# Attention, Fourier mixing and a split-precision feed-forward on one core: an instruction order written out by hand, and feed-forward blocks of 512 tokens

## The chip, the core and the metric

The kernel runs on one core of a Trainium2 chip. A core has five engines that each run their own instruction queue in order: TensorE (PE; its weight loads are listed apart as PEld), VectorE (DVE), ScalarE (ACT), GpSimd (POOL) and SyncE (SP), which only issues transfers. Engines wait for each other by semaphores. Matmuls write to PSUM, which has eight banks of 512 fp32 values per partition; everything else lies in SBUF. The metric is the device time of one execution in microseconds (us). The kernel before took 1088.26 us, the median of 3 runs (1086.99 to 1090.42).

## What is computed

```python
def reference(q, k, v, w1, w2):        # B=8, H=8, S=576, D=64
    k_p = k.reshape(B, H, 72, 8, D).mean(axis=3)       # keys and values pooled by 8
    v_p = v.reshape(B, H, 72, 8, D).mean(axis=3)
    attn = softmax(q @ k_p.T / sqrt(D)) @ v_p
    x = attn.transpose(0, 2, 1, 3).reshape(B, S, 512)
    u = x + real(fft(fft(x, axis=1), axis=2))          # over tokens, then over channels
    un = (u - u.mean(-1)) / sqrt(u.var(-1) + 1e-6)
    return u + relu(un @ w1) @ w2                      # 512 -> 2048 -> 512, weights in fp64
```

There are 8 x 576 = 4608 tokens.

## The kernel before

**Two kinds of work.** For each batch `fe(b)`, here called the front end, does the attention, the two Fourier transforms as matmuls with cosine and sine tables, the sum u and the layer norm. It leaves four tiles for the feed-forward: `unh` and `unl` (high and low part of the centred u, 4 channel tiles), `U` (u itself) and `rb` (the factor of the norm, which is multiplied in at the end). These hold 1152 tokens, two batches, as a ring. `ffn(ro, nb, to, f0, f1)` (L705) then does a block of `nb` tokens.

**A step of the feed-forward.** Step f does 128 of the 2048 hidden channels with 24 matmuls of `nb` columns: 12 at L731 into a PSUM tile `g` (high parts, `unl` with the high weights, `unh` with the low weights, for 4 channel tiles each), then ACT writes `hh` (relu, rounded, L735), DVE writes `hl` (the rest, L736), and 12 at L715 add to four PSUM tiles `acc`. The `g` matmuls of the next step stand ahead of the `acc` matmuls of this one. After the last step of a block DVE does two passes per `acc` tile (L745, L746), and SP stores the result.

**Blocks.** `blocks()` (L71) names them in the order in which they run: batch 0 in two halves of 288 tokens, steps 0 to 7 of both and then 8 to 15 of both; batches 1 to 6 in nine blocks of 384 tokens with 16 steps each; batch 7 in two halves of 288 tokens. That makes 64 steps of 288 columns and 144 of 384.

**Weights.** They come as fp64 words. `prep_w(n)` (L178) turns a piece into a high and a low part: two ACT passes (L193, L195), two DVE passes (L198, L199), the high part by ACT (L203), the low part by POOL (L204), which is stored to DRAM (L205). Every step then loads its two low parts again (`load_low`, L211; SBUF has no room for all of them). The tiles for this are seven buffers under the tag `w`.

**Idle matmuls.** `keep_busy` (L223) has PE multiply the identity by itself, with numbers of repeats from the table `BUSY` (L58), 61 in all; each is two records in the trace.

**What sets the order.** A scheduler decides from a model of times how the instructions of the generators are laid into each engine's queue; `advance` and `need` say how far the front ends and the weights run ahead of the feed-forward, and `issue_after` ties single ones to others. The constant tables are loaded by POOL's queue (L129 `ca`, for the channels, 1157 KB; L130 `cb`, for the tokens, 1445 KB).

Of the kernel before, what the change touches and what calls it, by code (L numbers as in the profile page):

```python
# [29 lines left out]

NAT = {0, 1}

NM = {0, 1}
# [3 lines left out]
PK = {1, 2, 3, 4, 5, 6, 7}  # L37
PV = {0}

EL = {1}  # L40

HZ = {0, 1}

DG = {0, 1}


UE = [4, 1, 0]
UL = [3, 3, 2]

AHEAD, LEAD, PACE = 11, 12, 0.65  # L50

THIRD = 18

TAIL0, TAIL1, NEXT, STEPS = 10, 11, 20, 10
# [3 lines left out]
BUSY = {"start": 8, "S3": 3, "S2": 7, "S0": 9, "S1": 4, "T3": 3, "R": 4, "X": 12, "A": 3, "M": 8}  # L58
# [8 lines left out]
def slot(b):  # L67
    return ((b + 1) % 2) * S
# [15 lines left out]
def tile_kernel(ctx: ExitStack, tc: tile.TileContext, qt, kt, vm, vr, w1, w2, cad, cbd, mkd, out):  # L84
# [5 lines left out]
    wide = w1.dtype != F32  # L90

    wls = [dp.tile([P, NFC, DM], F32, name=f"w{i + 1}l") for i in range(2)]

# [39 lines left out]
    pieces = [(i, f, 0, 4, None) for f in range(12) for i in (0, 1)] + [(0, f, 0, 4, None) for f in range(12, 16)]  # L133
    pieces = [(i, f, c, w, n % (3 if THIRD <= n < 24 else 2)) for n, (i, f, c, w, _) in enumerate(pieces)] + [(1, 12, 0, 4, 1), (1, 13, 0, 4, 1)]
    pieces += [(1, f, c, 2, None) for f in (14, 15) for c in (0, 2)]

    after = {}
    for m, x in enumerate(pieces):
        same = [n for n in range(m) if pieces[n][4] == x[4]]
        if x[4] is None:  # L140
            after.setdefault(same[-2] if len(same) >= 2 else 26, []).append(m)
        elif m > 1:
            after.setdefault(same[-1] if same else m - 4, []).append(m)
    staged = {}

# [15 lines left out]
    def load_w(n):  # L161
        if n >= len(pieces):
            return
        i, f, c, w, place = pieces[n]
        src = (w1, w2)[i][:, f, c * P:(c + w) * P]
        if not wide:
            st = wk.tile([P, DM], F32, tag="w", bufs=7, name="wraw")[:, 0:w * P]
            nc.sync.dma_start(st, src)
            staged[n] = st
            return  # L170
        if place is not None:
            st = wk.tile([P, 2 * DM], I32, tag=f"tail{place}", name="wst")
        else:
            st = wk.tile([P, DM], I32, tag="w", bufs=7, name="wraw")
        nc.sync.dma_start(st, src.bitcast(I32))
        staged[n] = st.rearrange("p (c m w) -> p c m w", m=P, w=2)

    def prep_w(n):  # L178
        if n >= len(pieces):
            return  # L180
        i, f, c, w, _ = pieces[n]
        cl = slice(c * P, (c + w) * P)
        if wide:
            st = staged.pop(n)
# [12 lines left out]
            with tc.issue_after(behind["E", 0].ins) if n == 3 else ExitStack():
                nc.vector.tensor_scalar(out=dh[:, :, :, 1], in0=halves[:, :, :, 3], scalar1=0x8000, scalar2=None, op0=ALU.bitwise_and)  # L198
            nc.vector.scalar_tensor_tensor(out=di, in0=hi, scalar=3, in1=di, op0=ALU.logical_shift_left, op1=ALU.bitwise_or)  # L199
        else:  # L200
            d0 = staged.pop(n)
        wh = high(i, f)[:, cl]
        nc.scalar.copy(out=wh, in_=d0)  # L203
        nc.gpsimd.tensor_tensor(out=d0, in0=d0, in1=raw(wh), op=ALU.subtract)  # L204
        nc.sync.dma_start(wls[i][:, f, cl], d0)  # L205
        for m in after.get(n, ()):
            load_w(m)
# [3 lines left out]
    def load_low(i, n):  # L211

        lows[i, n] = t = wk.tile([P, DM], F32R, tag="w", bufs=7, name=f"w{i + 1}low")
# [5 lines left out]
    turn, behind = [0], {}  # L219

    idle = pp.tile([P, 512], F32, tag="acc3", name="idle")

    def keep_busy(n, ins=None):  # L223

        with tc.issue_after(ins.ins) if ins else ExitStack():
            for _ in range(n):
                nc.tensor.matmul(idle[:, 0:P], lhsT=ident, rhs=ident, start=True, stop=True)

    def bank(b, name, late=False):
        tag = "fe"  # L230
        if b == 0 and not late:

            tags = ["g1", "acc0", "fe", "g1", "acc1", "acc2", "fe"] if turn[0] < 24 else ["g1", "acc0", "g1", "acc1", "acc2"]
            tag = tags[turn[0] % len(tags)]
            turn[0] += 1
# [7 lines left out]

    keep_busy(BUSY["start"])


    def fe(b):
        ro = slot(b)
        Ub = U[:, :, ro:ro + S]
        Xb = Ub if b == 1 else X  # L250
# [43 lines left out]
        def prep_v(gi, i):  # L294
            g = GROUPS[gi][i]
            if i == 0:
                prep_rem(gi)
# [634 lines left out]
```

## Time and profile before

| what | value |
|---|---|
| median of 3 runs | 1088.26 us (1086.99 to 1090.42) |
| profiled execution, its own time | 1088.63 us |
| its span, first to last instruction | 1086.9 us |
| PE busy | 1044.1 us (96% of the span) |
| DVE, ACT, POOL busy | 609.4, 415.0, 249.4 us |
| mean granted clock of TensorE | 0.981 |

The profiled execution took 1.7 us more than its span, and 0.4 us more than the median. PE is busy nearly all the time, so the share of busy time alone says little: what matters is where PE is not busy, where its clock is granted at half, and how long one matmul takes when nothing else is in the way. The span falls into the stretch up to the first `g` matmul (0 to 77.5 us), one with the feed-forward of batch 0 and the front end of batch 1 (to 200.3 us), one up to the first block of 384 (to 244.5 us), the nine blocks of 384 (to 976.4 us), the two last blocks of 288, and the end.

### The profile page before, as it was taken

Reading aid. Unit: us, or ns where it says so; the run is one execution under the profiler, and the core shown is the slowest. Engines: PE = TensorE matmul, PEld = TensorE weight load, DVE = VectorE, ACT = ScalarE, POOL = GpSimd, SP = SyncE. Lnnn points to the kernel's source line nnn. Section 1 sums busy time; section 2 is a strip of 40 time slices with the busy share of each in tenths; the row PEclk is TensorE's granted clock in tenths of the full one; section 3 lists DMA queues with packets and bytes.
Section 4 is the critical chain, followed back from the end, with each engine's and each line's share of the span. In section 5 each row is a group of like instructions: output and inputs, shape, how many; then the busy total and the mean of one; then the engine's idle time right before and its main releaser. Section 6 shows DMA issues by size and latency. Waiting matters only on the chain.

```text
span 1086.9 us, 17702 instructions
## 1 busy us (share of the span) xinstructions
PE 1044.1 (96%) x6606; PEld 1018.9 (94%) x6606; DVE 609.4 (56%) x1237; ACT 415.0 (38%) x1102; POOL 249.4 (23%) x249
## 2 busy tenths in 40 slices
PE   8848898999999999999999999999999999999997
PEld 7737788999999999999999999999999999999997
DVE  7686878856376455756277455656467434522212
ACT  6767764543143341443233341443324422311110
POOL 4464355312240032201240122300331101300000
PEclk9878998999999999999999999999999999999999
DMA  7767976675445454445444454445435334446563
GB/s 246 259 215 249 330 253 213 191 201 165 127 122 162 123 167 133 128 141 162 139 122 147 140 155 132 135 125 156 158 108 157 97 107 123 115 131 185 166 187 99
DMA packets 91878, 175.80 MB, mean 162 GB/s; under 512 B 10128, under 2 KB 17296, under 8 KB 91536
## 3 DMA queue, kind: packets, MB, share of 16 engines
q1 hardware_dynamic: 91504, 172.01, 51.7%
q0 software_dynamic: 288, 2.66, 0.6%
q8 instruction: 52, 0.85, 0.3%
q14 instruction: 34, 0.28, 0.1%
HBM read 156.81 MB, written 17.83 MB: 161 GB/s over the span
## 4 chain that ended last, share of the span: by engine, by line
PE 85%; DVE 5%; DMA 4%; ACT 2%; POOL 2%; issue 1%; SPq 0%; DVEq 0%; POOLq 0%; ACTq 0%
PE acc L715 35%; PE g L731 35%; PE psX L432 3%; PE psS L345 3%; PE psP L592 2%; DMA k<-in_kt 1%; PE psA L547 1%; PE psB L575 1%; PE psT L385 1%; PE psQ L592 1%; DVE wd L199 1%; POOL k L280 1%; DMA w2l<-wd 1%; DVE wd L198 1%; PE psR L408 1%
## 5 line engine op out<-in xcount | busy, mean ns | idle before, releaser
L735 ACT ACTIVATE hh<-g 128x384 fp32r<-128x384 f32 (+1 forms) x208 | 96.2, 463 | 305.4 <-PE g L731 285.6
L736 DVE SCALAR_TENSOR_TENSOR hl<-g,hh 128x384 fp32r<-128x384 f32 (+1 forms) x208 | 108.6, 522 | 185.0 <-ACT hh L735 179.4
L715 PE MATMUL acc<-hh,w2h 128*128 128x384 f32 (+1 forms) x832 | 190.5, 329 | 0.2 <-DVE U L746 0.2
L715 PE MATMUL acc<-hh,w2low 128*128 128x384 f32 (+1 forms) x832 | 186.8, 327 | 0.3 <-DMA w2low<-w2l 0.3
L715 PE MATMUL acc<-hl,w2h 128*128 128x384 f32 (+1 forms) x832 | 182.3, 328 | 1.1 <-DVE hl L736 1.1
L731 PE MATMUL g<-unh,w1low 128*128 128x384 f32 (+1 forms) x832 | 178.2, 329 | 1.6 <-DMA w1low<-w1l 1.6
L731 PE MATMUL g<-unl,w1h 128*128 128x384 f32 (+1 forms) x832 | 177.8, 328 | 1.0 <-DVE unl L633 1.0
L731 PE MATMUL g<-unh,w1h 128*128 128x384 f32 (+1 forms) x832 | 175.6, 328 | 0.0
L715 PEld LDWEIGHTS acc<-hh,w2h 128*128 128x128 f32 x832 | 143.1, 189 | 2.6 <-ACT hh L735 0.7
L715 PEld LDWEIGHTS acc<-hh,w2low 128*128 128x128 f32 x832 | 144.0, 189 | 0.6 <-DMA w2low<-w2l 0.5
L715 PEld LDWEIGHTS acc<-hl,w2h 128*128 128x128 f32 x832 | 141.4, 190 | 2.1 <-DVE hl L736 1.7
L731 PEld LDWEIGHTS g<-unh,w1low 128*128 128x128 f32 x832 | 141.0, 190 | 2.0 <-DMA w1low<-w1l 1.8
L731 PEld LDWEIGHTS g<-unl,w1h 128*128 128x128 f32 x832 | 140.7, 190 | 1.4 <-DVE unl L633 1.3
L731 PEld LDWEIGHTS g<-unh,w1h 128*128 128x128 f32 x832 | 140.7, 191 | 1.3 <-issue 0.8
L364 POOL TENSOR_TENSOR t<-t,sm 128x720 f32<-128x720 f32 x32 | 47.0, 1469 | 284.6 <-DVE sm L363 247.3
L280 POOL TENSOR_TENSOR k<-k 128x288 f32<-128x288 f32 (+1 forms) x56 | 42.3, 755 | 97.1 <-DMA k<-in_kt 73.3
L624 POOL TENSOR_TENSOR U<-X,U 128x576 f32<-128x576 f32 (+1 forms) x14 | 20.0, 1433 | 124.9 <-DVE X L608 124.9
L345 PE MATMUL psS<-kpb,q 128*128 128x144 f32 x280 | 43.2, 289 | 3.8 <-DVE X L608 2.1
L345 PEld LDWEIGHTS psS<-kpb,q 128*128 128x128 f32 x280 | 39.8, 191 | 4.2 <-issue 2.3
L349 DVE TENSOR_REDUCE mx<-psS 128x6 f32<-128x432 f32 (+1 forms) x64 | 33.1, 525 | 18.9 <-PE psS L345 18.6
L360 ACT ACTIVATE t<-t 128x720 f32<-128x720 f32 x30 | 24.1, 804 | 37.3 <-DVE t L358 37.0
L745 DVE TENSOR_TENSOR acc<-acc,rb 128x384 f32<-128x384 f32 (+1 forms) x60 | 29.0, 518 | 13.8 <-PE acc L715 13.5
(209 smaller groups left out, 1425.7 us busy)
## 6 DMA issues: line engine op xcount, KB each, us to landing
w1low<-w1l SPq DMA_DIRECT2D x208, 256.0 KB, 2.7
w2low<-w2l SPq DMA_DIRECT2D x208, 256.0 KB, 2.9
wst<-in_w SPq DMA_DIRECT2D x30, 512.0 KB, 4.7
q<-in_qt SPq DMA_DIRECT2D x28, 288.0 KB, 3.1
k<-in_kt SPq DMA_DIRECT2D x28, 288.0 KB, 2.9
v<-in_vm SPq DMA_DIRECT2D x28, 256.0 KB, 3.0
out<-U SPq DMA_DIRECT2D x18, 384.0 KB, 3.5
w1l<-wd SPq DMA_DIRECT2D x16, 256.0 KB, 4.4
```

Of the source, the lines that this page charges most:

```text
L280: nc.gpsimd.tensor_tensor(out=out if n == 1 else src[:, :, 0:n], in0=src[:, :, 0] if n == 1 else src[:, :, 0:n], in1=src[:, :, 1] if n == ...
L345: mm = nc.tensor.matmul(ps[:, c * W2J:(c + 1) * W2J], lhsT=q[:, r0:r0 + P], rhs=kpb[g % 2], start=True, stop=True)
L349: nc.vector.tensor_reduce(out=mx[:, c0:c0 + n], in_=pv, op=ALU.max, axis=AX.X, negate=(b, g) in SM)
L360: nc.scalar.activation(t, t, AF.Exp, scale=1.0 / 64.0)
L364: ins = nc.gpsimd.tensor_tensor(out=t, in0=t, in1=sm.unsqueeze(3).broadcast_to([P, 5, 2, J]), op=ALU.mult)
L432: last = nc.tensor.matmul(ps, lhsT=w, rhs=a, start=(i == 0), stop=(i == len(mm) - 1))
L592: nc.tensor.matmul(ps, lhsT=w, rhs=a, start=(i == 0), stop=(i == 6))
L715: nc.tensor.matmul(acc[e], lhsT=w[:, e], rhs=h, start=(f == f0 and x == 0), stop=(f == f1 - 1 and x == 2))
L731: nc.tensor.matmul(ps, lhsT=w[:, c], rhs=x[:, ti, cl], start=(n == 0), stop=(n == 11))
L735: nc.scalar.activation(hh, ps, AF.Relu)
L736: nc.vector.scalar_tensor_tensor(out=hl, in0=ps, scalar=0.0, in1=raw(hh), op0=ALU.max, op1=ALU.subtract)
L745: nc.vector.tensor_tensor(out=acc[e], in0=acc[e], in1=rb[:, cl], op=ALU.mult)
```

## The change

**Blocks.** Batch 0 keeps its halves of 288 tokens, now with steps 0 to 3 of both, 4 to 7 of both, then a block of batch 1's first 512 tokens with all 16 steps, then steps 8 to 15 of both halves. Batches 2 to 7 follow with one block of 512 tokens each. The 64 tokens that each of the batches 1 to 7 leaves over are stored to DRAM by `keep_rest` (four transfers a batch) and loaded again by `load_rest`; they make the last block, of 448 tokens. That makes 32 steps of 288 columns, 112 of 512 and 16 of 448.

**Order.** Every generator yields after each single instruction. Each has a letter: `A` to `H` are parts of batch 0's front end and `a` to `h` those of batch 1's, `s` to `q` those of batches 2 to 7, `y` the feed-forward, `x` the loads of low parts, `L` and `1` to `4` the weights' load, ACT, DVE, copy and subtraction with its store. A string of some 3,000 entries says which goes next and by how many instructions, and this is the order on all five queues; the scheduler is off.

**Smaller edits.** 61 idle matmuls become 8, at the start. The pass tiles `wd` of the weights get 5 buffers of their own, the tag `w` has 8 instead of 7. The low parts of weights with f below 8 stay in SBUF for their first use. For batches 2 to 7 two of the four last additions of a block go from DVE to POOL. In batch 0's front end the additions and the norm are done half by half.

```diff
+NB = 512
+RM = S - NB
-AHEAD, LEAD, PACE = 11, 12, 0.65
-BUSY = {"start": 8, "S3": 3, "S2": 7, "S0": 9, "S1": 4, "T3": 3, "R": 4, "X": 12, "A": 3, "M": 8}
+ORDER = """
+i5 A1 i2 A1 G3 A2 B1 L1 A1 B2 G2 L1 B1 A1 i1 G1 B1 A3 B1 G4 A1 G2 A1 G1 A1 B1 G1 A1 G1 12 i1 11 A1 B1 11 B2 21 C1 A1 C1 21 C1 i1 B2 i1 E2 D1
...
+WD, RW = 5, 8
...
-    r = [(slot(0) + h * HS, HS, h * HS, f, f + 8) for f in (0, 8) for h in range(2)]
-    for m in range(3):
-        r += [(i * 384, 384, S + m * RING + i * 384, 0, NFC) for i in range(3)]
-    return r + [(slot(7) + h * HS, HS, 7 * S + h * HS, 0, NFC) for h in range(2)]
+    r = [(0, slot(0) + h * HS, HS, h * HS, f, f + 4) for f in (0, 4) for h in range(2)]
+    r += [(1, slot(1), NB, S, 0, NFC)]
+    r += [(0, slot(0) + h * HS, HS, h * HS, 8, NFC) for h in range(2)]
+    r += [(b, slot(b), NB, S + (b - 1) * NB, 0, NFC) for b in range(2, B)]
+    return r + [(B, slot(6), (B - 1) * RM, S + (B - 1) * NB, 0, NFC)]
...
     def load_consts():
         nc.gpsimd.dma_start(ca, cad)
+        yield
         nc.gpsimd.dma_start(cb, cbd)
+        yield
...
+            low = wk.tile([P, DM], F32R, tag="w", bufs=RW, name=f"w{i + 1}low") if f < 8 else d0.bitcast(F32R)
+            nc.gpsimd.tensor_tensor(out=low, in0=d0, in1=raw(high(i, f)[:, cl]), op=ALU.subtract)
+            yield
+            nc.sync.dma_start(wls[i][:, f, cl], raw(low))
+            if f < 8:
+                lows[i, f + f // 4 * 4] = low
...
-    keep_busy(BUSY["start"])
+    keep_busy(8)
+    def keep_rest(b):
+        cl = slice(slot(b) + NB, slot(b) + S)
+        for t, r in zip((raw(unh), raw(unl), U), rests):
+            nc.sync.dma_start(r[:, :, b - 1], t[:, :, cl])
+            yield
+        nc.sync.dma_start(rests[3][:, 0, b - 1], rb[:, cl])
+        yield
...
+            u = U[:, e, cl]
+            v = raw(gt(2 + e, "v"))[:, 0:nb] if e < 2 and b > 1 else acc[e]
+            nc.vector.tensor_tensor(out=v, in0=acc[e], in1=rb[:, cl], op=ALU.mult)
+            yield
+            (nc.gpsimd if e < 2 and b > 1 else nc.vector).tensor_tensor(out=u, in0=u, in1=v, op=ALU.add)
+            yield
...
+    with tc.manual_schedule(engines=ENG):
+        for x in ORDER.split():
+            for _ in range(int(x[1:])):
+                assert go(x[0], True)
```

Three places show what the order does. On DVE, the stretch between the last sums of batch 0's inverse transform (`X<-X,psP`) and its first `unl`. Before (`mx`, `sm` and `t_3_723` belong to batch 1's softmax, `wd` to the weights):

```order
L607 TENSOR_TENSOR X<-X,psP_2_546 128x2x287
L608 TENSOR_TENSOR X<-X,psP_2_546 128x2
L349 TENSOR_REDUCE mx<-psS_2_0_771 128x6
L361 TENSOR_REDUCE sm<-t_3_723 128x10
L349 TENSOR_REDUCE mx<-psS_2_3_783 128x4
L198 TENSOR_SCALAR wd<-wst 128x512
L624 TENSOR_TENSOR U<-X,U 128x288 x2
L617 TENSOR_TENSOR s<-X 128x288
L624 TENSOR_TENSOR U<-X,U 128x288
L617 TENSOR_TENSOR s<-X 128x288
L624 TENSOR_TENSOR U<-X,U 128x288
L198 TENSOR_SCALAR wd<-wst 128x512
```

And now (both `L1212` rows belong to the first half alone):

```order
L1150 TENSOR_TENSOR X<-X,psP_2_571 128x2x287
L1152 TENSOR_TENSOR X<-X,psP_2_571 128x2
L1184 TENSOR_TENSOR U<-X 128x288 x2
L1158 TENSOR_TENSOR U<-X,psQ_1_584 128x288
L1160 TENSOR_TENSOR U<-X,psQ_1_584 128x288
L1206 TENSOR_TENSOR U<-X,U 128x288
L1208 TENSOR_TENSOR U<-X,U 128x288
L1212 TENSOR_TENSOR X<-U,psM_0_616 128x2x288 x2
L1220 TENSOR_TENSOR unl<-X,unh 128x288 x3
L1206 TENSOR_TENSOR U<-X,U 128x288
L1208 TENSOR_TENSOR U<-X,U 128x288
```

Batch 1's softmax, the weights' passes and the second half's additions no longer stand ahead of the first half's `unl`. On PE, from the means `psM` of batch 0 into the first step of the feed-forward, before:

```order
L345 MATMUL psS_2_0_771<-kpb_75,q_2_758 128x144 x3
L345 MATMUL psS_2_3_783<-kpb_75,q_2_758 128x144 x2
L638 MATMUL psM_569<-s,avg 128x288
L638 MATMUL psM_580<-s,avg 128x288
L227 MATMUL idle<-ident 128x128 x8
L385 MATMUL psT_3_823<-ident,t_3_723 128x128 x4
L731 MATMUL g_0_0_1478<-unh,w1h 128x288
```

And now:

```order
L1171 MATMUL psM_0_616<-U,avg 128x288
L1171 MATMUL psM_1_618<-U,avg 128x288
L1303 MATMUL g_0_0_655<-unh,w1h 128x288 x4
L827 MATMUL psS_3_3_665<-kpb_80,q_3_279 128x144 x2
L1303 MATMUL g_0_0_655<-unl,w1h 128x288 x4
L1303 MATMUL g_0_0_655<-unh,w1low 128x288 x4
```

The eight idle matmuls and batch 1's transposes are gone from between them, and batch 1's scores `psS_2` come after. On POOL, around the loads of the constant tables, before:

```order
L364 TENSOR_TENSOR t_0_218<-t_0_218,sm 128x720
L129 DMA ca<-in_cad 128x2314
L130 DMA cb<-in_cbd 128x2890
L308 MEMSET wlo 32x128
L204 TENSOR_TENSOR wd<-wd,w1h 128x512
L308 MEMSET wlo 32x128
L364 TENSOR_TENSOR t_1_287<-t_1_287,sm 128x720
```

And now:

```order
L858 TENSOR_TENSOR t_1_256<-t_1_256,sm 128x720
L894 MEMSET wlo 128x128
L782 TENSOR_TENSOR k_3_216<-k_3_216 128x72x2
L236 TENSOR_TENSOR w1low<-wd,w1h 128x512
L939 MEMSET U 128x576
L782 TENSOR_TENSOR ks<-k_3_216 128x72
L894 MEMSET wlo 128x128
L169 DMA ca<-in_cad 128x2314
L236 TENSOR_TENSOR w2low<-wd,w2h 128x512
L171 DMA cb<-in_cbd 128x2890
```

Both loads stand behind the last normalisation of batch 0 (`t_1`) and behind one or two subtractions of the weights.

## Rows read from the trace of the kernel before

**Rows 1.** Windows by stage: bounds, length, then the columns of the first line

```profile
core 0: us, PE busy (x) PEld busy (x) DVE busy (x) ACT busy (x) POOL busy (x), PEclk, DMA share, GB/s
0.00:77.50 77.50, 54.31 (x326) 46.53 (x327) 55.67 (x116) 51.27 (x149) 37.01 (x52) 0.88 0.71 237
77.50:200.30 122.80, 109.34 (x687) 98.34 (x686) 96.73 (x189) 79.91 (x208) 61.34 (x60) 0.91 0.80 258
200.30:244.50 44.20, 44.20 (x340) 43.86 (x339) 26.09 (x68) 18.85 (x53) 7.11 (x5) 1.00 0.66 194
244.50:976.40 731.90, 731.90 (x4480) 726.18 (x4479) 406.80 (x811) 251.78 (x663) 143.97 (x134) 1.00 0.45 136
976.40:1080.60 104.20, 104.20 (x782) 104.01 (x780) 21.29 (x49) 13.15 (x32) 0.00 (x0) 1.00 0.56 163
1080.60:1086.90 6.30, 0.14 (x2) 0.00 (x0) 2.79 (x8) 0.00 (x0) 0.00 (x0) 0.93 0.29 94
```

**Rows 2.** Chain of waits in the blocks of 384: start, length, what, matmuls

```profile
959.80 2.10 PE g L731 x12
961.90 2.11 PE acc L715 x12
```

**Rows 3.** Chain of waits in the last blocks of 288

```profile
1031.38 3.17 PE g L731 x24
1034.55 3.19 PE acc L715 x24
```

**Rows 4.** PE's groups by line and form: busy, mean ns, idle before

```profile
L715 PE MATMUL acc<-hh,w2h 128*128 128x384 f32 x576 | 137.7, 340 | 0.0
L227 PE MATMUL idle<-ident 128*128 128x128 f32 x122 | 18.8, 315 | 1.8 <-POOL ident masks.py:199 1.8
```

**Rows 5.** ACT's and DVE's evictions by form, 244.5 to 1080 us

```profile
L735 ACT ACTIVATE hh<-g 128x384 fp32r<-128x384 f32 x144 | 70.3, 488 | 198.7 <-PE g L731 186.0 <-PE acc L715 11.7
...
L736 DVE SCALAR_TENSOR_TENSOR hl<-g,hh 128x384 fp32r<-128x384 f32 x144 | 79.7, 553 | 97.2 <-ACT hh L735 91.8 <-PE acc L715 3.4
```

**Rows 6.** Timeline of DVE, first sum and first low part of batch 0

```profile
36.64 0.94 DVE L444 TENSOR_TENSOR X<-psX,X 128x288 f32<-128x288 f32 x2 [1.35 <-PE psX L432]
...
76.97 1.47 DVE L633 TENSOR_TENSOR unl<-X,unh 128x288 fp32r<-128x288 f32 x1
```

**Rows 7.** Window between these two rows, columns as in Rows 1

```profile
36.64:76.97 40.33, 23.10 (x151) 19.89 (x150) 34.08 (x73) 25.37 (x76) 20.94 (x23) 0.86 0.64 203
```

**Rows 8.** DVE's groups by form, 36.6 to 77 us

```profile
L199 DVE SCALAR_TENSOR_TENSOR wd<-wst,wd 128x512 int32<-128x512 int32 x6 | 4.4, 728 | 0.0
L198 DVE TENSOR_SCALAR wd<-wst 128x512 uint16<-128x512 uint16 x7 | 3.7, 532 | 2.1 <-ACT wst L193 2.1
L644 DVE TENSOR_TENSOR X<-U,psM 128x1152 f32<-128x1152 f32 x2 | 2.5, 1307 | 0.0
L277 DVE TENSOR_REDUCE vs<-v 128x64 f32<-128x512 f32 x3 | 2.0, 672 | 0.0
```

**Rows 9.** Timeline of POOL around the loads of constants

```profile
22.00 1.22 POOL L129 DMA_DIRECT2D ca<-in_cad  x1
23.22 0.53 POOL L130 DMA_DIRECT2D cb<-in_cbd  x1
...
27.60 1.39 POOL L364 TENSOR_TENSOR t<-t,sm 128x720 f32<-128x720 f32 x1 [0.20 <-DVE sm L363]
```

**Rows 10.** Transfers: queue, KB, median us to landing

```profile
cb<-in_cbd POOLq DMA_DIRECT2D x1, 1445.0 KB, 9.7
```

**Rows 11.** Windows with the clock at half, columns as in Rows 1

```profile
62.00:68.80 6.80, 3.66 (x12) 3.04 (x13) 6.80 (x18) 2.06 (x4) 3.48 (x3) 0.50 0.47 181
72.30:85.90 13.60, 8.19 (x34) 7.82 (x35) 10.10 (x13) 11.29 (x36) 9.57 (x8) 0.50 0.60 188
```

**Rows 12.** Timeline of the end

```profile
1080.38 1.56 DVE L745 TENSOR_TENSOR acc<-acc,rb 128x288 f32<-128x288 f32 x4 [1.86 <-PE acc L715]
1081.85 1.53 DVE L746 TENSOR_TENSOR U<-U,acc 128x288 f32<-128x288 f32 x4
```

More of the change, by code (lines that the diff above doesn't have):

```diff
@@ L209, in tile_kernel @@
     lows = {}
     def load_low(i, n):
-        lows[i, n] = t = wk.tile([P, DM], F32R, tag="w", bufs=7, name=f"w{i + 1}low")
+        lows[i, n] = t = wk.tile([P, DM], F32R, tag="w", bufs=RW, name=f"w{i + 1}low")
         nc.sync.dma_start(raw(t), wls[i][:, steps[n]])
     steps = [f for *_, f0, f1 in blocks() for f in range(f0, f1)]
[L219 to L227, printed above, removed]
@@ L229, in bank, with keep_busy @@
-    def bank(b, name, late=False):
[L230 to L235, printed above, removed]
+    def keep_busy(n):
+        idle = pp.tile([P, 512], F32, tag="acc3", name="idle")
+        for _ in range(n):
+            nc.tensor.matmul(idle[:, 0:P], lhsT=ident, rhs=ident, start=True, stop=True)
+    def bank(b, name, late=False):
+        tag = "fe" if b or late else ("g1", "acc0", "g1", "acc1", "acc2", "acc3")[BANKS.index(name[2] + name[4:]) % 6]
@@ L700, in fe, with go @@
-        yield
+                    yield
+            yield 1
+        yield from steady(b, st, Xb, Ub, load, load_v, load_rem, prep_k, prep_v, scores, transposes, values, halves)
+    counts, streams = {}, {}
+    def go(x, fine=False):
+        traced = nc.cur_bb.bb.instructions
+        n = len(traced)
+        while True:
+            r = next(streams[x], 0)
+            if r == 1:
+                counts[x] = counts.get(x, 0) + 1
+            if r == 0 or (len(traced) > n if fine else r == 1):
+                return r != 0
@@ new lines, in loads, with weights @@
+    def loads():
+        for n in range(len(pieces)):
+            if pieces[n][4] in (2, 3):
+                pull("F", 3)
+            same = [m for m in range(n) if pieces[m][4] == pieces[n][4]]
+            if pieces[n][4] is None:
+                pull("2", 27 if len(same) < 2 else same[-2] + 1)
+            elif same:
+                pull("2", same[-1] + 1)
+            load_w(n)
+            yield
+            yield 1
+    def weights(k):
+        for n in range(len(pieces)):
+            pull("L123"[k], n + 1)
+            yield from prep_w(n, "ADCS"[k])
+            yield 1
@@ new lines, in ready, with feed @@
+    def ready(f):
+        pull("4", 1 + (2 * f + 1 if f < 12 else (28, 29, 31, 33)[f - 12]))
+    def feed():
+        for n, blk in enumerate(blocks()):
+            it = ffn(*blk)
+            last = 2 * (blk[5] - blk[4]) - 1
+            for h in range(last + 1):
+                pull("H", 20 if n or h > 1 else 18)
+                if h == last:
+                    pull("H", 25)
+                if blk[0] == 1:
+                    pull("h", 25 if h == last else 20)
+                while next(it) is None:
+                    yield
+                yield 1
+            assert next(it, 0) == 0
@@ new lines, in low_loads, with later, consts @@
+    def low_loads():
+        for n in range(len(steps)):
+            ready(steps[n])
+            for i in range(2):
+                if (i, n) not in lows:
+                    load_low(i, n)
+                    yield
+            yield 1
+    def later(b, *needs):
+        n = 0
+        for r in fe(b):
+            for a, x, m in needs:
+                if a == n:
+                    pull(x, m)
+            yield r
+            n += r == 1
+    def consts():
+        yield from load_consts()
+        yield 1
@@ new lines, in tile_kernel @@
+    streams.update({str(k + 1): weights(k) for k in range(4)}, L=loads(), x=low_loads(), y=feed(),
+        s=later(2, (0, "a", 6), (0, "b", 6), (0, "c", 6), (0, "d", 6), (0, "g", 4), (2, "h", 6), (4, "f", 7), (6, "h", 16), (10, "h", 25), (22, "y", 64)),
+        t=later(3, (0, "s", 22), (2, "s", 25), (6, "s", 29), (10, "s", 32)), u=later(4), v=later(5), p=later(6), q=later(7), r=load_rest(), k=consts(), l=first(), i=initial())
+    with tc.manual_schedule(engines=ENG):
+        for x in ORDER.split():
+            for _ in range(int(x[1:])):
+                assert go(x[0], True)
```

1371 lines of the change are left out of this document (942 added, 429 removed).

## The prediction, made before the changed kernel had run

> **What bounds the kernel now.** I read the windows by stage first [rows 1]. The columns to compare are PE's busy time with the length, and the clock: in the blocks of 384 (244.5 to 976.4) PE is busy 731.90 of 731.90 us at clock 1.00, and so it is from 200.3 on and in the last blocks of 288. There only PE work counts. Before that two stretches are loose: up to the first `g` at 77.5 us PE is busy 54.31 us, from 77.5 to 200.3 it is busy 109.34 of 122.80 us at a mean clock of 0.91, and there DVE is busy 96.73 us with 189 instructions, the most after PE.
>
> The second view is the chain of waits, for the price of one matmul. The mean of a record (340 ns [rows 4]) is no price, since the records overlap; the chain's pieces lie end to end: 12 + 12 matmuls of 384 columns take 2.10 + 2.11 us [rows 2], 175.4 ns each, and 24 + 24 of 288 columns take 3.17 + 3.19 us [rows 3], 132.5 ns each. The difference of 42.9 ns for 96 columns is 0.447 ns a column.
>
> With these prices the span is taken apart. The feed-forward is 64 steps x 24 x 132.5 ns = 203.5 us and 144 x 24 x 175.4 ns = 606.2 us, together 809.7. What the blocks of 384 leave over is front ends: 731.9 - 606.2 = 125.7 us for 4480 - 3456 = 1024 records [rows 1], 0.123 us a record. Of the profile's 6606 PE records 4992 are feed-forward and 122 idle [rows 4], so a front end has 1492 / 8 = 186.5 records or 22.9 us, and batches 1 to 7 take 160.3. Then 1086.9 = 77.5 (up to the first `g`) + 809.7 + 160.3 + 6.3 (the end [rows 1, 12]) + 33.1, and these 33.1 us are lost between 77.5 and 200.3: 122.8 - 109.3 = 13.5 us PE was not busy; a mean clock of 0.91 is half clock for 18% of the stretch, 22 us, in which some 11 us were lost; the last 8 or so I can't place.
>
> **The change part by part.**
>
> Width of the blocks. By 0.447 ns a column from 384 upward a matmul of 512 costs 232.6 ns and one of 448 204.0 ns (estimates; no row has these widths). New: 32 x 24 x 132.5 = 101.8, 112 x 24 x 232.6 = 625.2, 16 x 24 x 204.0 = 78.3, together 805.3 us: 4.4 less. Bounds: if what a matmul of 384 takes over its columns at the clock (175.4 - 384/2.4 = 15.4 ns) is a fixed sum, 512 costs 228.7 ns and 2688 of them 10.5 us less than I count; if the price is proportional (175.4 x 512/384 = 233.9), 3.5 us more. The line through both measured widths lies between, and I take it. So the wide blocks are worth little by themselves: PE streams the same columns, in fewer pieces.
>
> A step of 512 lasts 24 x 232.6 ns = 5.6 us. Its `hh` and `hl` (0.488 and 0.553 us at 384 [rows 5], some 0.65 and 0.74 at 512) fit under the 12 `acc` matmuls that stand between a `g` and its use, 2.8 us. ACT waited 186.0 us for `g` and DVE 91.8 us for `hh` [rows 5], so they have room; cost 0, and without this cover 1.4 us a step.
>
> The first `g`. Between DVE's first sum of batch 0 (36.64) and its first `unl` (76.97) [rows 6] DVE is busy 34.08 of 40.33 us with 73 instructions, 0.467 each [rows 7]. By the order 26 of them leave this stretch: 7 weight passes (4 x 0.532 + 3 x 0.728 = 4.3), 3 reductions (2.0), 12 of batch 1's softmax and 4 additions of the second half (16 x 0.467 = 7.5); the two subtractions of the mean get half as long (2.5 to 1.25) [rows 8]. Five passes become nine of half the length, which I count as nothing. That is 15.0 us less, 19.1 us busy. Idle time was 6.3 us; it grows, since a step that waits for PE or ACT (sine and cosine sums go DVE, ACT, PE, DVE in turn) now has less to fill it. If it stays 6.3, the first `g` comes at 36.6 + 19.1 + 6.3 = 62; if it grows to 17, at 73. I take 67, 10.5 us earlier. What is late next is the table `cb`: it was issued at 23.22 and takes 9.7 us [rows 9, 10]; now it stands behind the normalisation that ran at 27.6 [rows 9] and two subtractions, which I put at some 38 us. It lands at 48 then, about when the first transform back needs it; each us later than 50 costs one.
>
> The idle matmuls. 122 records become 16. They ran where PE had nothing else, so their 18.8 us [rows 4] give nothing back; what they may cost is a rival below. In two stretches with sparse matmuls the clock was at half although they were there, 62.0 to 68.8 (PE busy 3.66 of 6.80) and 72.3 to 85.9 [rows 11].
>
> The stretch up to batch 1's block. It holds 16 half-steps (24 x 132.5 ns x 16 = 50.9 us) and batch 1's front end (22.9): PE needs 73.8 us. By the order DVE has 175 instructions from the first `unl` to batch 1's last, where the old stretch has 189; at the old mean of 96.73 / 189 = 0.512 us these are 89.6 us, more than PE's. DVE bounds this stretch, and its length lies between 82 (the instructions are shorter than the mean) and 114 us (DVE is busy no more than 96.73 of 122.8, as before). I take 92, near the busy time, since the softmax of batch 1 and the weights' passes stand one by one between the evictions and no long wait of DVE is left that I can see in the order. Then 18 us are lost there and not 33.1.
>
> Low parts that stay, more buffers, two additions on POOL, `keep_rest` and `load_rest`. All lie beside PE: the reloads of low parts load the DMA engines at 0.45 in the blocks of 384, POOL is busy 143.97 of 731.9 us there [rows 1], and the last block is loaded long before. Cost 0; uncovered, a late `load_rest` would cost one round of transfers of some 5 us.
>
> The end. The last block has 448 columns instead of 288 and its additions are split between two engines; four products and four sums took 1.56 and 1.53 us [rows 12]. I leave 6.
>
> Sum: 67 + 805.3 + 160.3 + 18 + 6 = 1056.6 us of span, and 1.7 around it: 1058.3. The profiled execution was 0.4 us over the median, which I ignore.
>
> **The rivals.**
>
> *The loose stretch stays as loose.* DVE's queue is written now, and each instruction in it waits for its own input with all others behind it. If DVE is busy no more than before, the stretch lasts 114 us: 22 more, 1080. For it: the old order had waits of all kinds there. Against: what is in the way is moved off, and the low parts are in SBUF already. If the first `g` stays at 77 too, 1088 to 1091: no change.
>
> *A matmul has a fixed cost.* Then the 2688 matmuls of 512 take 228.7 ns, 10.5 us less: 1048. For it: nothing but that only two widths are measured. Against: the two give a slope of 0.447 ns, above 1/2.4 = 0.417. By the Trainium skill, "TensorE: Matmul & The Clock Gate", section "Back-to-back issue gap", a lone matmul at full clock takes its columns over 2.4 plus 2.5 ns. That would be 162.5 ns for 384, where the chain shows 175.4, so this trace does not agree; with its 215.8 ns for 512 the sum would be 45 us lower, and I give that no weight.
>
> *The clock stays at half: slower.* Rows 11 show half clock after sparse work. Without 53 idle matmuls PE does less from 15 to 67 us, and in the next stretch it waits for DVE. If the clock is at half for three quarters of the stretch, PE's 73.8 us become 129 (+37 on my 92), and the transforms on the way to the first `g` (23.10 us of PE work before [rows 7], about 8 us of it in DVE's way) come 8 us later: 1103. It decides against the change from 30 us more than I count, which is half clock in some two thirds of the stretch. Against: in the old stretch it was at half only 18% of the time with 13.5 us of idle PE, and the feed-forward's matmuls are dense whenever they run. The same page, section "What's actually happening", says that the throttled state is the default and activity releases it; the rows at 62 to 69 and 72 to 86 us agree, and by that rule the idle matmuls were worth something.
>
> *The written order stops PE in the steady part: slower.* An eviction behind a waiting front-end instruction on ACT or DVE would hold up `acc`. The room is 2.8 - 1.4 = 1.4 us a step; a wait of 0.3 us in each of 128 wide steps costs 38: 1096. Against: no idle time of PE from 200 to 1080 before [rows 1], and the front ends stand a block ahead of their use.
>
> **How the numbers follow.** The forecast gets 0.55, with its own range of 1043 to 1073 (first `g` 62 to 73, stretch 82 to 100, width -10.5 to +3.5). The loose stretch gets 0.18 (a third of it with no gain at the first `g`), the fixed cost 0.13, the clock 0.08, the stopped steady part 0.06. The range that leaves out no more than 2 in 10 reaches from 1038 (fixed cost with the shorter stretch) to 1081. Within 0.3% (3.3 us, about what can be told from no change here) lies the worst end of the loose stretch, 0.05; slower are the last two rivals but for their mild cases, 0.10; faster the rest, 0.85.
>
> **What would show it.** The first `g` at 62 to 73 us, and which wait stands before it (a wait for `cb` would be my step of the tables gone wrong). In the chain, 12 matmuls of 512 in 2.79 us (2.74 under a fixed cost). The first `g` of 512 columns at about 159 us, with DVE busy near 90 of the 92 us before it; at 180 it is the first rival. The windows with clock 0.50: some 20 us of them before 160, or over 50. From there on PE busy without a gap to the end. The prediction is wrong if PE waits in the steady part, or if the time before the first wide block is not shorter by 20 us or more for its work.

## The result, and the profile after

The changed kernel took 1057.71 us, the median of 4 runs (1057.01 to 1059.13), against 1089.34 us before (1086.99 to 1091.26, the three runs above and one more): a ratio of 0.9712, 95% interval 0.9688 to 0.9736. The forecast was 1058 us. The profiled execution took 1057.01 us with a span of 1055.3 us, so the sum of 1056.6 us of span was 1.3 us too high. That the sum fits this well is luck: the traces show below that terms were off by 3 to 9 us and cancel, and that one edit was priced at nothing which, in the changed order, the experiments price at some 18 us and more.

The windows by stage of the changed kernel, with the columns of [rows 1]; the bounds are the first `g` (58.8), the first `g` of 512 columns (148.2), the first of 448 (970.9) and the last matmul (1049.0):

```profile
0.00:58.80 58.80, 37.58 (x202) 30.75 (x202) 47.08 (x95) 39.61 (x109) 24.50 (x40) 0.90 0.73 252
58.80:148.20 89.40, 84.67 (x577) 78.97 (x578) 81.62 (x176) 69.37 (x197) 52.25 (x54) 0.97 0.72 245
...
148.20:970.90 822.70, 819.23 (x4188) 687.93 (x4187) 464.70 (x883) 291.68 (x742) 182.05 (x172) 1.00 0.40 130
970.90:1049.00 78.10, 78.06 (x385) 71.82 (x383) 13.90 (x23) 8.73 (x16) 2.52 (x3) 1.00 0.32 101
```

Against [rows 1] the stretch up to the first `g` is 18.7 us shorter, of the 31.6 us by which the whole span is. In the next one three engines are in heavy use: PE is busy 84.67 of 89.40 us at clock 0.97, DVE 81.62, ACT 69.37; before it was 109.34 of 122.80 at 0.91. From 148.2 us on PE is without work for 3.5 us only.

The price of a matmul, from the chain of waits at the change from 512 to 448 columns (start, length, what, matmuls):

```profile
959.85 2.79 PE acc L1289 x12
962.64 2.79 PE g L1303 x12
...
975.87 2.44 PE acc L1289 x12
978.31 2.43 PE g L1303 x12
```

2.79 / 12 = 232.5 ns for 512 columns (forecast 232.6) and 2.435 / 12 = 202.9 ns for 448 (204.0): the line through the two widths of [rows 2, 3] holds, and a fixed cost per matmul (228.7 ns) does not. No front end runs beside these steps.

What PE waited for, over the whole of the changed kernel (us in total, times, longest):

```profile
PE psA L1065 <- DMA ca<-in_cad: 4.8, 1, 4.8
PE g L1303 <- ACT unh L1217: 4.3, 1, 4.3
PE psT L926 <- POOL t L858: 4.2, 1, 4.2
PE psS L827 <- ACT kpb L801: 3.3, 4, 1.5
...
PE acc L1289 <- DVE U L1323: 1.5, 3, 0.6
```

No wait of the feed-forward for a low part is left. The longest wait is for the table `ca`, not `cb`, on the way to the first `g`. Of the waits shown, the first three and part of the fourth lie ahead of the first `g`.

The first row of batch 0's sums on DVE, its first `unl`, and between them two sums that are dear (start, length):

```profile
31.68 0.46 DVE L985 TENSOR_TENSOR X<-psX,X 128x288 f32<-128x288 f32 x1 [0.82 <-PE psX L967]
...
51.08 2.54 DVE L1184 TENSOR_TENSOR U<-X 128x288 f32<-128x288 f32 x2
...
58.90 1.19 DVE L1220 TENSOR_TENSOR unl<-X,unh 128x288 fp32r<-128x288 f32 x3
```

These answer to [rows 6]: the way from the first sum to the first `unl` is 27.2 us, not 40.3, and it also begins 5.0 us earlier.

### The profile page after: what moved, and what is told of

It is laid out like the page before. It is cut to its first block, busy times and chain, and to the rows that moved or that the text cites. A ratio compares the mean times of both kernels' runs of the same rounds, so it can differ in the third digit from the quotient of the medians.

```text
span 1055.3 us, 14747 instructions
## 1 busy us (share of the span) xinstructions
PE 1019.5 (97%) x5348; PEld 869.5 (82%) x5348; DVE 609.1 (58%) x1177; ACT 409.4 (39%) x1062; POOL 262.5 (25%) x269
## 4 chain that ended last, share of the span: by engine, by line
PE 81%; DVE 10%; POOL 3%; ACT 2%; DMA 2%; issue 1%; SPq 0%; DVEq 0%; POOLq 0%; ACTq 0%
PE g L1303 34%; PE acc L1289 34%; PE psS L614 3%; PE psX L694 2%; PE psP L287 2%; PE psA L396 1%; DVE wd L227 1%; PE psB L412 1%; PE psQ L287 1%; PE psT L651 1%; DMA ca<-in_cad 1%; DVE wd L225 1%; DMA k<-in_kt 1%; PE psA L1065 1%; POOL t L858 0%
## 5 line engine op out<-in xcount | busy, mean ns | idle before, releaser
L1310 DVE SCALAR_TENSOR_TENSOR hl<-g,hh 128x512 fp32r<-128x512 f32 (+2 forms) x160 | 101.1, 633 | 217.4 <-ACT hh L1308 216.8
L1308 ACT ACTIVATE hh<-g 128x512 fp32r<-128x512 f32 (+2 forms) x160 | 88.3, 552 | 293.6 <-PE g L1303 292.7
L1289 PE MATMUL acc<-hh,w2h 128*128 128x512 f32 (+2 forms) x640 | 170.5, 376 | 2.2 <-DVE U L1323 1.5
L1289 PE MATMUL acc<-hl,w2h 128*128 128x512 f32 (+2 forms) x640 | 168.0, 373 | 0.0
L1289 PE MATMUL acc<-hh,w2low 128*128 128x512 f32 (+2 forms) x640 | 167.9, 373 | 0.0
L1303 PE MATMUL g<-unh,w1h 128*128 128x512 f32 (+2 forms) x640 | 162.9, 376 | 4.3 <-ACT unh L1217 4.3
L1303 PE MATMUL g<-unl,w1h 128*128 128x512 f32 (+2 forms) x640 | 162.4, 375 | 0.3 <-DVE unl L1220 0.3
L1303 PE MATMUL g<-unh,w1low 128*128 128x512 f32 (+2 forms) x640 | 162.5, 376 | 0.0
L1289 PEld LDWEIGHTS acc<-hh,w2h 128*128 128x128 f32 x640 | 113.9, 188 | 21.6 <-DVE U L1323 2.5
L1289 PEld LDWEIGHTS acc<-hh,w2low 128*128 128x128 f32 x640 | 115.0, 188 | 19.0
L553 POOL TENSOR_TENSOR k<-k 128x288 f32<-128x288 f32 (+1 forms) x48 | 31.7, 660 | 54.4 <-DMA k<-in_kt 29.9
L621 ACT ACTIVATE t<-t 128x720 f32<-128x720 f32 x24 | 19.3, 805 | 41.4 <-DVE t L619 41.4
```

The costliest lines, as they stand in the source:

```text
L553: nc.gpsimd.tensor_tensor(out=out if n == 1 else src[:, :, 0:n], in0=src[:, :, 0] if n == 1 else src[:, :, 0:n], in1=src[:, :, 1] if n == ...
L621: nc.scalar.activation(t, t, AF.Exp, scale=1.0 / 64.0)
L1289: nc.tensor.matmul(acc[e], lhsT=w[:, e], rhs=h, start=(f == f0 and x == 0), stop=(f == f1 - 1 and x == 2))
L1303: nc.tensor.matmul(ps, lhsT=w[:, c], rhs=x[:, ti, cl], start=(n == 0), stop=(n == 11))
L1308: nc.scalar.activation(hh, ps, AF.Relu)
L1310: nc.vector.scalar_tensor_tensor(out=hl, in0=ps, scalar=0.0, in1=raw(hh), op0=ALU.max, op1=ALU.subtract)
```

## The experiments

All were timed against the kernel before. Its medians beside these runs were 1088.15 to 1088.43 us, against 1089.34 beside the changed kernel, so a difference of about 1 us between two runs says little. Differences are of medians from the changed kernel's 1057.71 us.

**The scheduler decides again.** Blocks, buffers and kept low parts stay.

```diff
-    with tc.manual_schedule(engines=ENG):
+    with ExitStack():
```

> The changed kernel with the scheduler deciding each engine's order again; blocks, buffers and kept low parts stay as changed. Theory (the written order brings the gain, by the first g at 58.8 us and the packed stretch of 89.4 us up to the first block of 512): the first g comes at 68 to 80 us, the first block of 512 starts at 165 to 190 us instead of 148, and the time is 1072 to 1095 us. Rival (the new blocks and the kept low parts bring it, the order is only a way to write it down): within 5 us of the changed kernel's 1057.7.

Measured: 1156.64 us, 99 us more (ratio to before 1.0628, 1.0596 to 1.066). The first `g` came at 86.5 us, the first block of 512 at 195.1.

```profile
0.00:86.50 86.50, 47.71 (x217) 38.33 (x217) 66.10 (x126) 57.63 (x166) 39.38 (x61) 0.74 0.73 248
86.50:195.10 108.60, 87.81 (x564) 78.98 (x564) 85.59 (x174) 63.45 (x171) 51.54 (x49) 0.92 0.58 197
195.10:1075.00 879.90, 849.91 (x4211) 711.51 (x4211) 447.40 (x858) 281.63 (x712) 171.50 (x158) 0.96 0.38 115
```

The last row ends a little into the last block. The new blocks alone are not the gain; without the written order they come out slower than the kernel before. But the loss is larger than either theory said, and 52 of the 99 us arise after the first block of 512 has begun (PE is idle for 30 us there, and its mean granted clock is 0.96). The generators were rewritten to be laid out by the string, and it may be that their plain text is no good order for the scheduler; that was not tested. So this run shows that the new kernel needs its written order, not by how much that order beats the old one.

**The low parts go through DRAM again.** The low parts of weights with f below 8 are stored and reloaded for their first use also. The loads are issued where the step asks for them.

```diff
-            low = wk.tile([P, DM], F32R, tag="w", bufs=RW, name=f"w{i + 1}low") if f < 8 else d0.bitcast(F32R)
+            low = d0.bitcast(F32R)
...
-            if f < 8:
-                lows[i, f + f // 4 * 4] = low
```

> The changed kernel in which every low part is stored and loaded again, also for its first use (16 parts, 32 transfers more in the stretch up to the first block of 512). Theory (DVE binds that stretch, the transfers lie beside it): -1 to +2 us. Rival (the stretch is dense because the low parts are in SBUF): PE's g waits for w1low again, and the time is 6 us or more longer.

Measured: 1075.48 us, 17.8 more (0.9885, 0.9863 to 0.9908). My theory falls: PE waited 14.2 us for them, and the first block of 512 began at 165.5 us, 17.3 later. The wait in total, and then the longest of the three with the transfers that SP issued ahead of it:

```profile
PE g L1301 <- DMA w1low<-w1l: 14.2, 3, 8.7
107.25 6.21 SPq L205 DMA_DIRECT2D wst<-in_w  x2
113.55 0.38 SPq L238 DMA_DIRECT2D w1l<-wd  x1
114.03 0.38 SPq L246 DMA_DIRECT2D w1low<-w1l  x1
118.53 1.33 PE L1301 MATMUL g<-unh,w1low 128*128 128x288 f32 x4 [8.67 <-DMA w1low<-w1l]
```

The load of the low part (L246) was issued at 114.03 us and was there when PE went on at 118.53. Ahead of it in SP's queue stood a store and two loads of weights' words (L205), the second of which waited until 113 us. SP waited little for stores in this run, 3.8 us at L246. So the loss could have come from issuing the loads late, and the next run issues each right behind its store:

```diff
-                lows[i, f + f // 4 * 4] = low
+                load_low(i, f + f // 4 * 4)
```

> The changed kernel in which the 16 low parts are again stored and loaded back for their first use, but each load is issued by SP directly behind its store, long before the step that needs it (in the run before, the loads were issued where the steps stand, and it took 17.8 us more). Theory (the loss there came from loads that were issued late; transfers as such lie beside PE): 0 to 4 us longer than the changed kernel's 1057.7. Rival (the way through DRAM costs whenever it is taken, since SP waits for each store to land, some 3 to 4 us, with the other loads queued behind it): 8 to 18 us longer.

Measured: 1085.64 us, 27.9 more (0.9976, 0.9965 to 0.9988): more than either theory said, and nearly the whole gain is gone. Issuing early is worse than issuing late. The waits of SP's queue up to 180 us in this run:

```profile
SPq L248 <- DMA w2l<-wd: 38.0, 8, 11.0
SPq L248 <- DMA w1l<-wd: 32.7, 8, 5.6
```

L248 is the load of a low part. It waits for the store to land, 70.7 us in 16 waits, 4.4 us each, and every transfer behind it in SP's queue waits too: ACT then waited 19.3 us for `wst`, the weights' words, in the stretch (0.7 in the changed kernel), and the first `g` itself was 6.6 us late. The last run of the three copies the low part by a transfer from SBUF to SBUF, so that bytes, transfers and buffers are as in the run before but nothing waits for a store:

```diff
-                lows[i, f + f // 4 * 4] = low
+                lows[i, f + f // 4 * 4] = t = wk.tile([P, DM], F32R, tag="w", bufs=RW, name=f"w{i + 1}low")
+                nc.sync.dma_start(raw(t), raw(low))
```

> The run with the loads issued at once, but each low part is copied by a transfer from the tile in SBUF and not loaded back from DRAM: the same 16 transfers of 256 KB into the same buffers, without SP's wait for the store to land (which was 38.0 + 32.7 us for 16 stores there). Theory (SP's wait in the written order is what costs, with the weights' loads queued behind it): 0 to 4 us longer than the changed kernel's 1057.7. Rival (the extra transfers, or the buffers that are held longer, cost): 10 us or more longer.

Measured: 1061.01 us, 3.3 more (0.9743, 0.9724 to 0.9763). Of SP's waits for stores 3.1 us are left of 70.7, and the longest items are now the subtraction itself, which the stores waited for anyway, and a pass of DVE:

```profile
SPq L238 <- POOL wd L236: 35.3, 15, 6.7
SPq L205 <- DVE wd L227: 28.2, 10, 6.4
```

So 24.6 of the 27.9 us go with SP's waits (the transfers behind them and the low parts themselves come late), and about 3 with the transfers and buffers. That the load has to wait for the landing is what the Trainium skill states in "DMA: Bandwidth & Descriptors", section "Two DMAs through the same engine are not ordered": only the completion semaphore of the first orders a second that depends on it. SP waits in this way in the run with the loads issued at once; the price, 4.4 us for each of 16, is that run's.

**More work for DVE, for ACT and for PE, in the stretch from the first `g` to the first block of 512.** Each run adds instructions to one engine there, and changes nothing else in the program.

```diff
+            for _ in range(2 if 9 <= n < 27 else 1):
                 nc.vector.tensor_scalar(out=dh[:, :, :, 1], in0=st.bitcast(U16)[:, :, :, 3], scalar1=0x8000, scalar2=None, op0=ALU.bitwise_and)
```

> The changed kernel with one of DVE's two passes issued twice for 18 pieces of the weights (those prepared from 66 to 145 us): 18 x 0.46 to 0.7 us = 8 to 12 us more of DVE's work in the stretch of 89.4 us in which it is busy 81.6. Theory (DVE binds the stretch): the first block of 512 starts 5 to 12 us later and the time is 5 to 12 us longer. Rival (PE's 84.7 busy us or the chain of dependences bind it, and DVE's 7.8 idle us take the passes up): 0 to 3 us longer.

```diff
+            for _ in range(2 if 9 <= n < 27 else 1):
                 nc.scalar.activation(dh[:, :, :, 0], st.bitcast(U8)[:, :, :, 3], AF.Copy, scale=1.0 / 32.0, bias=-15.5 / 32.0)
```

> The changed kernel with one of ACT's two passes issued twice for the same 18 pieces: 18 x 0.66 to 0.78 us = 12 to 14 us more of ACT's work in the stretch in which it is busy 69.4 of 89.4 us. Theory (DVE binds, ACT has 20 us of room): 0 to 5 us longer. Rival (ACT is as much in the way, by the order of its queue): 8 to 14 us longer.

```diff
+                    for m in range(6 if b == 0 and f < 8 and n == 0 else 1):
-                    nc.tensor.matmul(ps, lhsT=w[:, c], rhs=x[:, ti, cl], start=(n == 0), stop=(n == 11))
+                        nc.tensor.matmul(ps, lhsT=w[:, c], rhs=x[:, ti, cl], start=(n == 0), stop=(n == 11 or (b == 0 and f < 8 and n == 0 and m < 5)))
```

> The changed kernel with the first matmul of each of the 16 early half-steps of batch 0 issued six times instead of once: 80 x 132.5 ns = 10.6 us more of PE's work in the stretch up to the first block of 512 (PE is busy 84.7 of 89.4 us there). Theory (PE, ACT and DVE are each near full, so that any of them lengthens the stretch by what is added): 7 to 11 us longer. Rival (DVE and ACT bind it and PE follows): 0 to 4 us longer.

| run | added to the engine | time | more than the changed kernel | ratio to before |
|---|---|---|---|---|
| DVE twice | 11.9 us (93.5 for 81.6) | 1068.05 | 10.3 | 0.9816 (0.9792 to 0.9839) |
| ACT twice | 13.1 us (82.5 for 69.4) | 1067.65 | 9.9 | 0.9806 (0.9784 to 0.9827) |
| PE more | 10.6 us (80 matmuls at 132.5 ns) | 1062.43 | 4.7 | 0.9763 (0.9743 to 0.9782) |

The stretch in the first two runs, with the columns of [rows 1], DVE's run first, and then ACT's:

```profile
59.00:159.00 100.00, 90.03 (x574) 83.85 (x575) 93.51 (x192) 69.19 (x197) 52.25 (x54) 0.91 0.67 218
```

```profile
59.00:159.00 100.00, 89.11 (x579) 82.53 (x580) 81.83 (x178) 82.54 (x215) 50.32 (x54) 0.93 0.65 219
```

DVE's work comes out nearly whole, as the theory had it. ACT's does too, against the theory: it had 20 us of idle time and took up only 3 of the 13. Idle time between the waits of a queue in fixed order was no room for more work here. PE, the busiest of the three, took up about half, which lies between the two theories. So all three bind; DVE and ACT alike, as far as these runs can tell them apart, and PE less.

Two things limit this. A part of the price is the clock: for as many matmuls as before PE is busy 90.03 and 89.11 us in these rows instead of 84.67, at a mean granted clock of 0.91 and 0.93 instead of 0.97. So some 4 to 5 of the 10 us are PE's own work at half clock, between longer waits. And both doubled passes stand in the one chain that prepares a weight (ACT, DVE, ACT, POOL), so a fuller engine is not told apart from a longer chain; in neither run, though, does the feed-forward wait for a weight in this stretch.

**The table `ca` earlier.** POOL issues it ahead of the normalisation of `t_0`.

```diff
-D1 a1 C1 E2 12 21
+D1 a1 k1 C1 E2 12 21
...
-a1 G2 k1 41 31 L1
+a1 G2 41 31 L1
```

> The changed kernel with the load of ca moved up in POOL's queue, ahead of the normalisation of t_0, so that it is issued at about 21.5 us instead of 30.6. Theory (PE's wait of 4.8 us for ca lies on the way to the first g): the wait is gone, the first g comes 2 to 4 us earlier, the time is 2 to 4 us shorter. Rival (the transfers already run at 300 to 400 GB/s from 20 to 33 us, so ca pushes other loads back, and DVE's own queue is as late): -1 to +3 us.

Measured: 1056.24 us, 1.5 less (0.97, 0.9682 to 0.9718, which overlaps the changed kernel's interval), between what the two theories said. The wait for `ca` is gone, but the first `g` came at 58.5 us, 0.3 earlier: PE waits for ACT's `unh` in its place.

```profile
PE psA L1062 <- ACT unh L1008: 4.6, 2, 3.9
PE g L1300 <- ACT unh L1214: 4.3, 1, 4.3
```

**Idle matmuls again in the two waits.** 16 ahead of the first `psA` and 14 ahead of the first `g`.

```diff
+    def busy_again():
+        for n in (16, 14):
+            idle = pp.tile([P, 512], F32, tag="acc1", name="idle")
+            for _ in range(n):
+                nc.tensor.matmul(idle[:, 0:P], lhsT=ident, rhs=ident, start=True, stop=True)
+            yield
```

> The changed kernel with idle matmuls again in PE's two long waits on the way to the first step: 16 ahead of the first psA (wait of 4.8 us) and 14 ahead of the first g (wait of 4.3 us). Theory (taking them out cost nothing, DVE and ACT are in the way): -1 to +1 us. Rival (the clock at half from 40 to 43 and from 58 to 63.5 us holds PE up, and the idle matmuls give it back): the clock stays at full there, 2 to 4 us shorter.

Measured: 1056.90 us, 0.8 less (0.9712, 0.9692 to 0.9731): no difference. In the changed kernel the clock is at half just behind these waits (0.52 from 40 to 43 us, and the first two rows below). In this run it is 1.00 in both places and falls only later, to 0.77 and 0.73, behind 3.4 us in which PE was busy for 1.21 us (61.2 to 64.6). The first `g` comes 1.0 us earlier, at 57.86, but the first block of 512 does not: 148.37 us against 148.24. The changed kernel first, then this run:

```profile
57.80:61.20 3.40, 2.37 (x9) 2.23 (x10) 3.37 (x7) 2.52 (x6) 1.34 (x2) 0.50 0.00 0
61.20:64.60 3.40, 3.40 (x18) 3.40 (x18) 3.37 (x6) 0.78 (x3) 1.03 (x2) 0.59 0.02 5
```

```profile
64.60:68.00 3.40, 2.12 (x9) 1.89 (x10) 3.40 (x8) 3.33 (x9) 2.32 (x3) 0.77 0.34 91
68.00:71.40 3.40, 3.40 (x22) 3.40 (x21) 3.40 (x6) 1.64 (x4) 1.56 (x2) 0.73 1.00 331
```

**Three edits ahead of the first `g` together.** `ca` early, 14 idle matmuls, and POOL's subtractions `w1low` and `w2low` of the third pair moved behind POOL's first `unl`.

```diff
-H5 31 41 ... H4 11 41 H7 L1 H3 y1 ... 41 y1
+H5 31 ... H4 11 H7 L1 H3 z1 y1 ... y1
...
+H2 44
```

> The changed kernel with three edits ahead of the first g: ca's load early (as in the run on it, 1.5 us), 14 idle matmuls in the wait before the first g, and POOL's two subtractions of the third pair of low parts moved behind its first unl, since DVE's two sums at 51.08 us took 2.54 us beside them instead of some 0.8. Theory (each is on the way to the first g): the first g at 56 to 57.5 us, 1.5 to 4 us shorter than the changed kernel's 1057.7. Rival (the next wait takes the place of each, and the held wd buffers delay ACT): -0.5 to +2 us.

Measured: 1056.91 us, 0.8 less (0.971, 0.9693 to 0.9726): no difference. The first `g` did come 1.65 us earlier, at 57.18, and DVE's two sums took a third of their time:

```profile
51.15 0.83 DVE L1188 TENSOR_TENSOR U<-X 128x288 f32<-128x288 f32 x2
```

But the first block of 512 began at 150.9 us, 2.6 later than in the changed kernel: what was gained ahead of the first `g` was lost in the next stretch. There PE is busy for only 0.75 and 1.12 us in the two stretches of 3.4 us from 61.2 to 68.0, and the clock is granted at 0.50 from 64.6 to 71.4 us, where the changed kernel has 1.00. The result is nearer to the rival than to the theory; which of its two reasons it was stays open.

**Width alone, on the kernel before.** 12 blocks of 288 for batches 1 to 6.

```diff
-        r += [(i * 384, 384, S + m * RING + i * 384, 0, NFC) for i in range(3)]
+        r += [(i * HS, HS, S + m * RING + i * HS, 0, NFC) for i in range(4)]
...
-    free = {1: 0, 2: 64, 3: 128, 4: 160, 5: 224, 6: 256, 7: 320}
+    free = {1: 0, 2: 64, 3: 128, 4: 192, 5: 256, 6: 320, 7: 384}
```

The second pair follows from the first: the steps are counted anew.

> The kernel before with batches 1 to 6 in 12 blocks of 288 tokens instead of 9 of 384, to price the width alone. Theory (0.447 ns a column and 3.8 ns a matmul): 3 x 16 x 24 x (4 x 132.5 - 3 x 175.4) ns = 4.4 us longer, 1091 to 1095 us against 1088.4. Rival (narrow steps leave too little cover for hh and hl beside the front ends, 1.6 us instead of 2.1): PE waits in the steady part, 10 us or more longer.

Measured: 1096.98 us, a ratio to before of 1.0073 (1.0047 to 1.0098), 5.1 to 10.7 us more. The sign is the theory's; its 4.4 us lie just below the interval. PE does not wait in the steady part (729.48 of 730.00 us busy from 250 to 980), so the rival fails; waits of `g` for `w1low` rose from 1.6 to 5.3 us early on, and the scheduler laid out a new order, so the run does not measure the width's share alone.

## Why the prediction came out right, step by step

**The width.** Right to 0.1 ns for 512 columns and 1.1 ns for 448, in steps with no front end beside them.

**The first `g`.** Forecast 67, measured 58.8. Of the 8.2 us, 5.0 are the first sum, which I left at 36.6 and which came at 31.7. The rest is the way from there: I took 19.1 us busy and 11.3 idle, and DVE was busy 23.5 of 27.2 us. The idle time did not grow, it fell to 3.7 us. So two errors of 4.4 and 7.6 us cancel in part.

Of the 4.4 us of busy time that I had not counted, 1.7 come from what runs beside an instruction: the two sums at 51.08 took 2.54 us next to POOL's subtractions, 0.83 when these were moved. POOL in the changed kernel:

```profile
50.57 1.29 POOL L236 TENSOR_TENSOR w1low<-wd,w1h 128x512 fp32r<-128x512 f32 x1
51.82 1.49 POOL L236 TENSOR_TENSOR w2low<-wd,w2h 128x512 fp32r<-128x512 f32 x1
```

The Trainium skill says in "SBUF — State Buffer", section "Who interferes with whom", that a DVE instruction with two SBUF inputs contends with a GpSimd instruction that reads SBUF; these two runs agree.

Another 1.7 us are the way of counting. Instructions of DVE overlap, as in the kernel before here:

```profile
37.50 0.45 DVE L445 TENSOR_TENSOR X<-psX,X 128x288 f32<-128x288 f32 x1
37.86 0.45 DVE L444 TENSOR_TENSOR X<-psX,X 128x288 f32<-128x288 f32 x1
```

The second starts 0.36 us after the first, which lasts 0.45, so a mean duration is more than an instruction adds to a full queue. By the starts in the trace, what I took off had filled some 13.3 us and not 15.0. It is the fault that I had avoided for PE. The last us is open.

**The tables.** I named `cb` as what is late next. It was `ca`, issued at 30.6 and there 9.5 us later, for which PE waited 4.8 us:

```profile
30.58 9.48 DMA ca<-in_cad
```

And that wait was hardly a price: without it the first `g` came 0.3 us earlier.

**The idle matmuls.** Nothing that can be told was lost without them, or gained with 30 of them back. The rival on the clock needed some 50 us at half clock; behind the first `g` there were about 5, up to 64.6 us, and none afterwards up to the first block of 512. Ahead of it a mean clock of 0.90 makes some 12, so that the 17 in all are near the 20 that the forecast named.

**The stretch up to the first block of 512.** Forecast 92, measured 89.4, and here too two errors cancel. DVE's 176 instructions (I had counted 175) took 81.62 us, 0.464 each and not 0.512, and DVE was idle for 7.8 us where the forecast left it 2.4. So its sign, DVE busy near 90 of the 92 us, did not come true. That DVE binds the stretch was half the truth, as the three runs with added work show: ACT binds as much, and PE is fullest.

**The low parts.** This step failed: "the reloads of low parts load the DMA engines at 0.45" and "Cost 0". I looked at the transfers' share and not at SP, whose queue is in fixed order as well and issues the weights' loads. In the changed order the 16 low parts cost 18 to 28 us if they go through DRAM. With loads issued at once nearly all of it goes with SP's waits for the stores; with loads issued late it is PE that waits, 14.2 us, and the longest of these waits is for a load that was queued behind others in SP. I got the right sum because I took the stretch's length from DVE's busy time, which holds only as long as SP is not in the way. In the kernel before, SP's loads of low parts waited for stores 13.7 us up to 200 us:

```profile
SPq L214 <- DMA w2l<-wd: 9.8, 6, 4.4
...
SPq L214 <- DMA w1l<-wd: 3.9, 4, 1.8
```

The old order had far less of these waits than the 70.7 us above; what keeping the parts would have been worth there was not run.

**The rest.** From the first block of 512 to the last matmul I had 805.3 + 160.3 - 50.9 - 22.9 = 891.8 us, and it took 900.8. PE was idle for 3.5 us of them, 2.7 of these up to 175 us; by the prediction's own words a wait of PE in the steady part is a sign that it is wrong, and so much of it is. The other 5.5 us are not dearer front ends. My 0.123 us a record was what the feed-forward at the chain's price left over. Counted in the traces from one start to the next, a front end's record takes 0.118 us before and 0.120 now. It is the feed-forward that takes longer where front ends run: a matmul of 384 columns takes 176.9 ns on average before, where the chain shows 175.4, and one of 512 takes 236.7 now (with PE's waits), where it shows 232.5. From 850 us on, with no front end left, the mean is the chain's price. So in this stretch the feed-forward was some 13 us more than I counted and the front ends some 4 us less. Why matmuls start later beside a front end is open.

The end took 6.3 us (forecast 6). With -8.2, -2.6, +9.0 and +0.3 the errors add up to the 1.3 to 1.5 us that the sum was off. Put in the prediction's own terms, 1055.3 - 58.8 - 805.3 - 160.3 - 6.3 = 24.6 us are lost behind the first `g`, against 33.1 before and 18 in the forecast. More was gained ahead of the first `g` than I said, and less behind it.

**The rivals.** The loose stretch did not come about, but two experiments made it (165.5 and 176.8 us for the first block of 512), with the low parts' way through SP's queue and not DVE as the reason. The fixed cost is excluded. Batch 1's block between batch 0's halves, which gives the late weights time, was not tried the other way round, so what its place is worth by itself stays open. No run shows either what single moves in the order, the five buffers for `wd`, the halves in batch 0's front end or the additions on POOL are worth.

## What to carry to other kernels

- The queue that issues transfers keeps its order like the others: here a load that depended on a store put the store's landing time, 4.4 us on average, ahead of everything queued behind it. Look at its waits before a round trip through DRAM is priced by its bytes.
- When several engines are each some 80 to 95% busy in one stretch, idle time there need not be a reserve. Adding one small operation per engine shows in three runs which of them binds; look at the granted clock in these runs too, since PE may also run slower when it waits more (0.91 and 0.93 above instead of 0.97).
- A price per matmul from the chain of waits at two widths carries to a third, for steps with nothing beside them; a busy time counted from mean durations doesn't carry as well, since durations overlap and the neighbours change.

## What the runs showed of the hardware that was not expected

The first two front ends multiply plain fp32 tiles. Their matmuls of 288 columns show as two records each, and at full clock two records take 0.49 us from start to start, 242 ns each, where a matmul of 288 columns on the rounded type takes 132.5 ns [rows 3]:

```profile
24.18 0.65 PE L966 MATMUL psX<-ah,wh 128*128 128x288 f32 x2
24.67 0.65 PE L967 MATMUL psX<-R,wlo 128*128 128x288 f32 x2
25.15 0.65 PE L966 MATMUL psX<-ah,wh 128*128 128x288 f32 x2
```

Batch 1's front end has 32 such records, from 92.0 us to 115.3, so 32 x 109.5 ns = 3.5 us of PE's work in the stretch up to the first block of 512 were missing from a price taken from rounded tiles. They lie ahead of that block, so they are no part of the 9.0 us behind it. The kernel before has such records too.
